# Attention with a shared key/value head and a Fourier block: probability-times-value bursts over six, five and five key chunks, with half sums kept in DRAM

## The chip, the cores and the metric

The kernel runs on one core of one Trainium2 chip. The metric is the device time of one execution in microseconds (us), lower is better. TensorE (PE) multiplies matrices, VectorE (DVE), ScalarE (ACT) and GpSimd (POOL) work on vectors, SyncE (SP) issues the DMAs. In the profile PEld stands for PE's weight loads, which overlap its matmuls, and a "q" behind an engine's name for its sequencer.

## What is computed

Two independent results stand side by side in the output. The left half is attention with 32 heads of 32 columns over 2048 positions, where all heads share one key and one value head. The right half is the real part of a two-dimensional Fourier transform, written as matrix products.

```python
# left half; x: 1 x 2048 x 1024
q = (x @ wq).reshape(B, S, H, Dh).transpose(0, 2, 1, 3)
k, v = x @ wk, x @ wv
scores = jnp.einsum("bhqd,bkd->bhqk", q, k) * (Dh ** -0.5)
p = softmax(scores, axis=-1)
o = jnp.einsum("bhqk,bkd->bhqd", p, v)
a = o.transpose(0, 2, 1, 3).reshape(B, S, H * Dh) @ wo
# right half; its own x
a_, b_ = einsum("bsd,ed->bse", x, dft_hid_re), einsum("bsd,ed->bse", x, dft_hid_im)
y = einsum("ts,bse->bte", dft_seq_re, a_) - einsum("ts,bse->bte", dft_seq_im, b_)
```

## The kernel before

**Products of three.** The projections, the Fourier stages and the output product are "groups". A group sums 8 blocks of 128 rows (stage one of the Fourier block: 4) into one PSUM bank `psb`; each block is three matmuls, since both operands are split into a high and a low part (`rh`, `rl` and `mh`, `ml`) to keep the precision. One such matmul is called a fill here. Operands come through two lines (`RL` for the right side, `ML` for the left) of four steps: load by SP (`r`, `m`), combination of two or three loaded tiles by POOL (`comb`), rounding to the high part (`hi_r`, `hi_m`) and subtraction to the low part (`lo`), on POOL after the start. Each step has a lead, counted in fills ahead of the operand's use, and `pump` issues what is due after every fill. A load can start when a buffer of the tile is free: three for the first source, two for the second; a third source had tiles of the pool `hp`.

**Stage two.** Seven products in turn (`PRODUCTS`), each of two halves of eight groups. The first half's sums are kept in eight tiles `h` of the pool `hp`; in the second half DVE adds the bank to `h`, and POOL adds `h` to the running results `y`, which are loaded from DRAM before (`load_y`, six buffers) and stored behind it.

**Attention.** It goes through 32 units, a unit being 4 heads by 512 queries, and each unit through 32 steps. A step of the main loop issues, in this order: the scores of a later unit (two matmuls `pss`, the row maxima by DVE into `nm`, and one step later their exponential sums by ACT); the exponentials of this unit (`expo`: two matmuls `pst` of 128 keys against 1024 query columns, and ACT's exponential into a tile `p`); now and then a burst; and the step's share of fills. The scores come with their row's logarithm already subtracted: query tiles `qst` have two spare rows, 96 and 97, that hold it, and the keys `kst` hold ones there. The query tile is taken from a pool of three, and POOL clears rows 96 to 127 in every unit (`open_unit`). The logarithms of a unit are made in small steps at fixed places (`LSE`): `lse_1`, `lse_1b`, `lse_2` on DVE and ACT, a transpose on PE (`lse_3`), and DMAs into the spare rows (`lse_4`, tile `mt`); in steps of the main loop these are 21, 22, 24, 26 and 28.

**Bursts.** `pv(u, k)` multiplies the tiles `p` of four chunks of 128 keys with the values, each for four heads, in four column groups of the array, and sums them in a bank; DVE adds the bank to `ov`. A burst follows every eighth step, and `level` spreads the fills over the seven steps in between, so that their sum up to a burst is as `goal` says. Nine tiles `p` are enough for this. `aside` takes a few fills more if a group is just begun or nearly done.

**Order.** Every engine runs its instructions in the order in which the program issues them; the fills between the matmuls of attention are set by `take`. SP is a queue of its own: a load that waits for a free buffer holds up all DMAs behind it. All instructions are issued through one helper, so the profile gives them all the same line, L66, and they are told apart by the names of their tiles.

Of the kernel before, what the change touches and what calls it, by code (L numbers as in the profile page):

```python
# [8 lines left out]
F32 = mybir.dt.float32  # L9
F32R = mybir.dt.float32r  # L10
# [6 lines left out]
P = 128  # L17
# [3 lines left out]
DH = 32  # L21
W = 512
NG = 8
NQ = 4
NC = 16
# [62 lines left out]
def tile_kernel(ctx: ExitStack, tc, xT, wq, wkv, wo, xbT, wT, cT, out):  # L88
# [40 lines left out]
    mp = pool(ctx, "mp", NM, side="right")  # L129
    yp = pool(ctx, "yp", NY, side="right")  # L130
    op = pool(ctx, "op", 2, side="right")
    hp = pool(ctx, "hp", 1, side="right")

    def move(q, to, of):
        q.dma_start(to.bitcast(F32), of.bitcast(F32))


    class Line:
# [6 lines left out]
        def may(self, k):  # L145
            i = self.n[k]
            if i >= len(self.items):
                return False
            if k == 0:
                return i < min(self.n[3] + self.nstage, self.n[1] + self.nstage - 1)  # L150
            if i >= self.n[k - 1]:
                return False
            if k == 2 and i >= self.nring:
                return self.items[i - self.nring].last < pos["fill"]
            return True
# [23 lines left out]
    def load_r(it):  # L179
        if it.pre or it.t:  # L180
            return
        it.t = []
        for n, (ap, _) in enumerate(it.srcs):
            if n < 2:
                it.t.append(r0p.tile([P, W], F32, name=f"r{n}", bufs=NR0 - n))
            else:
                it.t.append(spare(0, 5))
            sp.dma_start(it.t[-1], ap())

    def load_m(it):  # L190
        if it.pre:
            return
        it.t = []
        for n, (ap, _) in enumerate(it.srcs):
            a = ap()
            if n < 2:
                t = m0p.tile([P, 4, P], F32, name=f"m{n}", bufs=NM0 - n)
            else:
                t = spare(5, 3).rearrange("p (a b) -> p a b", a=4)
            it.t.append(t[:, :a.shape[1], :a.shape[2]])  # L200
            sp.dma_start(it.t[-1], a)

    turn = {0: 0, 5: 0}

    def spare(first, n):

        turn[first] += 1
        return hp.tile([P, W], F32, name=f"h{first + turn[first] % n}")

    def comb(it):  # L210
        if it.pre:
# [105 lines left out]
    def store(to, of, key=None):  # L317
        def go():
            move(sp, to, of)
            if key:  # L320
                ready.add(key)
        soon(go)
# [159 lines left out]
    hs = {}  # L482

    def have(key, ap):
        assert key in ready, key
        return ap

    def stage2():
        seen, total = {}, {}
        for _, _, outs in PRODUCTS:  # L490
            for t, e, _ in outs:
                total[t, e] = total.get((t, e), 0) + 1
        for mt, nt, outs in PRODUCTS:
            for half in range(2):
                R = [Item([(lambda s=s, k=k: have((k, s), s_d[k][s]), -1 if nt == SUB and i else 1) for i, k in enumerate(nt)])
                     for s in range(half * 8, half * 8 + 8)]
                for k in range(8):
                    left = []
                    for q in range(2):
                        s0 = half * 8 + q * 4  # L500
                        left.append(Item([(lambda a=a, k=k, s0=s0: cT[a[0], a[1] * 8 + k, :, s0:s0 + 4], a[2]) for a in mt]))
                    if half == 0:
                        def post(ps, k=k):
                            hs[k] = hp.tile([P, W], F32, name=f"h{k}")
                            dve.tensor_copy(hs[k], ps)
                        yield Group(left, R, post)
                        continue
                    ys = []
                    plan = []
                    for t, e, sg in outs:  # L510
                        n = seen.get((t, e, k), 0)
                        seen[t, e, k] = n + 1
                        it = None
                        if n:
                            it = Item([(lambda t=t, e=e, k=k: y_d[t][e][k], 1)])
                            ys.append(it)
                        r0 = (t * 8 + k) * P
                        to = out[r0:r0 + P, D + e * W:D + (e + 1) * W] if n + 1 == total[t, e] else y_d[t][e][k]
                        plan.append((sg, it, to))

                    def post(ps, k=k, plan=plan):
                        h = hs[k]
                        dve.tensor_add(h, h, ps)
                        for sg, it, to in plan:
                            if it is not None:
                                (gp.tensor_add if sg > 0 else gp.tensor_sub)(it.y, it.y, h)
                                store(to, it.y)
                            elif sg > 0:
                                store(to, h)
                            else:  # L530
# [39 lines left out]
    rest += [o_group(b, t, e, ws) for e, ws in ((1, w1), (0, w0)) for b in range(NQ - 1) for t in range(4)]  # L570
    add(start + rest)

    qsp = pool(ctx, "qsp", 3)
    pp = pool(ctx, "pp", 9)
    sm = pool(ctx, "sm", 2)
    onp = pool(ctx, "onp", 1)

# [7 lines left out]
    def open_unit(u):  # L585
        b, g = units[u]
        assert ("q", b, g) in ready
        q = qsp.tile([P, 4, W], F32R, name="qst")
        gp.memset(q[96:P].bitcast(F32), 0.0)
        for r, src in enumerate((qh_d, ql_d, qh_d)):  # L590
            move(sp, q[r * DH:(r + 1) * DH], src[b][g].rearrange("(h d) c -> d h c", d=DH))
        qst[u] = q
        nm[u] = sm.tile([P, 10, NC], F32, name="nm")
# [64 lines left out]
    def expo(n):  # L658
# [5 lines left out]
            te.matmul(ps[:, a], kst[:, c * P:(c + 1) * P], qst[u][:, 2 * hp_ + a], start=True, stop=True)  # L664
        act.activation(pt[u, c, hp_], ps, AF.Exp)

    def pv(u, k):

        aside()
        ps = bank("psb")  # L670
        for c in range(4 * k, 4 * k + 4):
            for h in range(4):
                te.matmul(ps[h * DH:(h + 1) * DH], v[:, c], pt[u, c, h // 2][:, h % 2], start=c == 4 * k, stop=c == 4 * k + 3)
        if k == 0:
            ov[u] = onp.tile([P, W], F32, name="ov")
            dve.tensor_copy(ov[u], ps)
        else:
            dve.tensor_add(ov[u], ov[u], ps)
        cur["at"] += 1
        if k == NC // 4 - 1:  # L680
            b, g = units[u]
            hi_ = onp.tile([P, W], F32R, name="oh")
            lo_ = onp.tile([P, W], F32R, name="ol")
            lse["out"] = hi_, lo_

# [29 lines left out]
    TURN = 6  # L715
    LSE = {1: (lse_1,), 2: (lse_1b,), 4: (lse_2,), 8: (lse_4,)}

    room = [(lambda t=t, k=k: t[:, k]) for t in [pp.tile([P, 2, W], F32, name="p") for _ in range(9)] for k in range(2)]
    room += [(lambda t=t: t) for t in [hp.tile([P, W], F32, name=f"h{k}") for k in range(8)]]
# [21 lines left out]
    def goal(n):  # L741
        return PRO + (FILL - PRO - LAST - MORE * (total - QUIET)) * n // total + MORE * max(n - QUIET, 0)


    def level(n):
        k, r = divmod(n, 8)
        if r == 0:
            return
        left = goal((k + 1) * 8) - pos["fill"]
        take(left - left * (7 - r) // (8 - r))  # L750

    for n in range(total):
        u, r = divmod(n, SU)
        if n == total - 12:
            w1 = wo_set(1)
            add([o_group(NQ - 1, t, e, ws) for e, ws in ((0, w0), (1, w1)) for t in range(4)])
        score_step(n + SU + LEAD)
# [12 lines left out]
    pv(len(units) - 1, 3)  # L770
    while ends:
        ends.pop(0)()
    hi7, lo7 = lse["out"]
# [64 lines left out]
```

## Time and profile before

| | before |
|---|---|
| runs, median (lowest to highest) | 2794.53 us (2789.01 to 2796.99), 3 runs |
| profiled execution | 2791.25 us |
| its span, first to last instruction | 2789.3 us |
| mean granted clock of PE | 0.998 |
| busy: PE, ACT, POOL, DVE | 99%, 78%, 59%, 58% |
| share of the DMA engines' time | 51.6% |

The span is one execution. "Busy" counts the time in which an engine has an instruction under way; PE's matmuls overlap, and PE is hardly ever idle. The largest groups of PE's instructions (mean length of one, which contains the overlap):

```profile
L66 PE MATMUL psb<-rh,mh 128*128 128x512 f32 (+1 forms) x1852 | 730.4, 394 | 9.7 <-ACT rh L66 8.3
...
L66 PE MATMUL pss<-kst,qst 128*128 128x512 f32 x2048 | 657.1, 402 | 1.3 <-ACT pss L66 1.2
L66 PE MATMUL pst<-qst,kst 128*128 128x512 f32 x2048 | 649.5, 398 | 4.4 <-DMA qst<-mt 3.6
...
L66 PE MATMUL psb<-p,v 128*32 128x512 f32 x4096 | 466.3, 596 | 0.0
```

A row reads: line, engine, operation, output tile from input tiles, shapes, number; busy us and mean ns of one; idle time of the engine just before them, and what ended it. The trace has each matmul of a burst twice, 32 for the 16 that the program issues.

### The profile page before, as it was taken

How to read it: one execution, taken by the hardware profiler on the slowest of the kernel's cores; microseconds unless marked ns; L12 is line 12 of the kernel's file. 1: busy time of each engine (PE TensorE's matmuls, PEld its weight loads, DVE VectorE, ACT ScalarE, POOL GpSimd, SP SyncE). 2: the span in 40 equal slices, each digit the busy share in tenths (PEclk: the TensorE clock that was granted, in tenths of full speed). 3: DMA queues.
4: the chain of work that ended last, by engine and by line, in shares of the span. 5: the costliest groups of instructions: out<-in, count | busy, mean ns of one | idle time of the engine just before them, and what ended most of it. 6: DMA issues, size and time to landing. Idle time of an engine off the chain costs nothing.

```text
span 2789.3 us, 40153 instructions
## 1 busy us (share of the span) xinstructions
PE 2763.8 (99%) x13904; PEld 1932.7 (69%) x13904; DVE 1624.4 (58%) x1864; ACT 2181.4 (78%) x3151; POOL 1651.0 (59%) x1622
## 2 busy tenths in 40 slices
PE   8999999999999999999999999999999999999999
PEld 5876767667666767666676767667676767676666
DVE  6766666666676665555555655555565555555411
ACT  4578888888788888888888888878888888888740
POOL 3755534665535538767686567798887885640110
PEclk9999999999999999999999999999999999999999
DMA  7544325766576554545453454555564552554455
GB/s 253 197 140 129 110 103 174 242 213 203 189 237 212 171 175 156 162 144 153 143 189 104 129 167 139 160 198 162 163 193 150 167 160 80 159 163 140 126 166 173
DMA packets 304203, 459.87 MB, mean 165 GB/s; under 512 B 32128, under 2 KB 97152, under 8 KB 304000
## 3 DMA queue, kind: packets, MB, share of 16 engines
q1 hardware_dynamic: 304000, 457.30, 51.6%
q8 instruction: 110, 1.80, 0.3%
q14 instruction: 93, 0.76, 0.1%
HBM read 351.54 MB, written 104.60 MB: 164 GB/s over the span
## 4 chain that ended last, share of the span: by engine, by line
PE 96%; DMA 1%; DVE 1%; ACT 1%; issue 0%; POOL 0%; SPq 0%; ACTq 0%; POOLq 0%; DVEq 0%
PE psb L66 61%; PE pss L66 18%; PE pst L66 17%; DMA p<-in_xT_dram 0%; DVE nm L66 0%; ACT pss L66 0%; SPq L66 0%; DVE rl L66 0%; ACT p L66 0%; DMA r<-s 0%; ACT rh L66 0%; DMA qst<-mt 0%; DMA ql<-ql 0%; DMA r<-in_xT_dram 0%; POOL ml L66 0%
## 5 line engine op out<-in xcount | busy, mean ns | idle before, releaser
L66 DVE TENSOR_REDUCE nm<-pss 128x1 f32<-128x1024 f32 x1024 | 1252.7, 1223 | 591.2 <-PE pss L66 590.3
L66 ACT ACTIVATE p<-pst 128x1024 f32<-128x1024 f32 x1024 | 1052.2, 1028 | 463.8 <-PE pst L66 461.3
L66 ACT ACTIVATE pss<-pss,nm 128x1024 f32<-128x1024 f32 x1024 | 1112.9, 1087 | 67.3 <-DVE nm L66 65.9
L66 PE MATMUL psb<-rh,mh 128*128 128x512 f32 (+1 forms) x1852 | 730.4, 394 | 9.7 <-ACT rh L66 8.3
L66 PE MATMUL psb<-rh,ml 128*128 128x512 f32 (+1 forms) x1852 | 730.1, 394 | 2.2 <-POOL ml L66 2.2
L66 PE MATMUL psb<-rl,mh 128*128 128x512 f32 (+1 forms) x1852 | 728.5, 393 | 0.3 <-DVE rl L66 0.3
L66 PE MATMUL pss<-kst,qst 128*128 128x512 f32 x2048 | 657.1, 402 | 1.3 <-ACT pss L66 1.2
L66 PE MATMUL pst<-qst,kst 128*128 128x512 f32 x2048 | 649.5, 398 | 4.4 <-DMA qst<-mt 3.6
L66 PEld LDWEIGHTS pss<-kst,qst 128*128 128x128 f32 x2048 | 372.2, 188 | 184.7 <-issue 102.3
L66 POOL TENSOR_TENSOR ml<-m,mh 128x512 fp32r<-128x512 f32 x340 | 438.8, 1291 | 48.2 <-ACT mh L66 40.4
L66 PE MATMUL psb<-p,v 128*32 128x512 f32 x4096 | 466.3, 596 | 0.0
L66 PEld LDWEIGHTS pst<-qst,kst 128*128 128x128 f32 x2048 | 377.4, 188 | 112.2 <-ACT p L66 20.8
L66 PEld LDWEIGHTS psb<-rh,mh 128*128 128x128 f32 (+1 forms) x1852 | 346.7, 187 | 95.9 <-ACT rh L66 9.0
L66 PEld LDWEIGHTS psb<-rh,ml 128*128 128x128 f32 (+1 forms) x1852 | 346.6, 187 | 86.7 <-POOL ml L66 3.5
L66 PEld LDWEIGHTS psb<-rl,mh 128*128 128x128 f32 (+1 forms) x1852 | 346.7, 187 | 84.5 <-DVE rl L66 1.4
L66 PEld LDWEIGHTS psb<-p,v 128*32 128x32 f32 x4096 | 120.0, 109 | 276.6 <-issue 265.6
L66 POOL CAST mh<-m 128x512 fp32r<-128x512 f32 x339 | 208.1, 614 | 166.0 <-PE psb L66 145.3
L66 POOL TENSOR_TENSOR r<-r,r 128x512 f32<-128x512 f32 x112 | 144.4, 1289 | 271.6 <-DMA r<-s 135.2
L66 POOL CAST rh<-r 128x512 fp32r<-128x512 f32 x214 | 131.5, 614 | 262.0 <-PE psb L66 144.9
L66 POOL TENSOR_TENSOR rl<-r,rh 128x512 fp32r<-128x512 f32 x214 | 276.2, 1291 | 3.9
L66 POOL TENSOR_TENSOR m<-m,m 128x512 f32<-128x512 f32 x192 | 247.9, 1291 | 28.7 <-DMA m<-in_xbT_dram 20.6
L66 DVE TENSOR_TENSOR ov<-ov,psb 128x512 f32<-128x512 f32 x96 | 66.0, 688 | 272.0 <-PE psb L66 272.0
(68 smaller groups left out, 929.5 us busy)
## 6 DMA issues: line engine op xcount, KB each, us to landing
m<-in_cT_dram SPq DMA_DIRECT2D x384, 256.0 KB, 3.7
r<-s SPq DMA_DIRECT2D x192, 256.0 KB, 4.3
y<-y SPq DMA_DIRECT2D x96, 256.0 KB, 4.6
r<-in_wT_dram SPq DMA_DIRECT2D x80, 256.0 KB, 3.7
m<-in_xbT_dram SPq DMA_DIRECT2D x80, 256.0 KB, 4.2
y<-u SPq DMA_DIRECT2D x80, 256.0 KB, 2.8
m<-in_wq_dram SPq DMA_DIRECT2D x64, 256.0 KB, 3.0
qst<-qh SPq DMA_DIRECT2D x64, 256.0 KB, 5.5
```

Source lines behind the costliest of these rows:

```text
L66: return lambda *a, **k: self.tc.keep_in_program_order(f(*a, **k))
```

## The change

A unit's 16 key chunks are cut at 0, 6, 11 and 16: three bursts a unit, at steps 12, 22 and 0 of the next, and `level` spreads the fills up to the next of these steps. Thirteen tiles `p` hold six chunks and one step. The room for four more tiles is that of `hp`, which goes: the half sums of stage two are copied to a tile of the output pool, stored to DRAM, and loaded in the second half as one more item of the `y` line; third sources share the second source's two buffers, and an item with three sources (or the one behind it) is loaded only after the item ahead has been combined. The three query tiles are named once; POOL clears the spare rows in the first three units alone, and later units get zeros into rows 96 and 97 by a small DMA from rows of `kst` that stay zero.

```diff
-    hp = pool(ctx, "hp", 1, side="right")
@@ class Line, may
             if k == 0:
+                if self.n[1] < i and any(len(it.srcs) > 2 for it in self.items[i - 1:i + 1] if it.srcs):
+                    return False
                 return i < min(self.n[3] + self.nstage, self.n[1] + self.nstage - 1)
@@ load_r
-            if n < 2:
-                it.t.append(r0p.tile([P, W], F32, name=f"r{n}", bufs=NR0 - n))
-            else:
-                it.t.append(spare(0, 5))
+            k = min(n, 1)
+            it.t.append(r0p.tile([P, W], F32, name=f"r{k}", bufs=NR0 - k))
             sp.dma_start(it.t[-1], ap())
@@ load_m
...
+            k = min(n, 1)
+            t = m0p.tile([P, 4, P], F32, name=f"m{k}", bufs=NM0 - k)
@@ stage2
-        for mt, nt, outs in PRODUCTS:
+        for f, (mt, nt, outs) in enumerate(PRODUCTS):
+            hs = [dram.tile([P, W], F32, name=f"hs_{f}_{k}") for k in range(8)]
...
-                        def post(ps, k=k):
-                            hs[k] = hp.tile([P, W], F32, name=f"h{k}")
-                            dve.tensor_copy(hs[k], ps)
+                        def post(ps, k=k, hs=hs, f=f):
+                            o = op.tile([P, W], F32, name="qh")
+                            dve.tensor_copy(o, ps)
+                            store(hs[k], o, ("h", f, k))
...
-                    ys = []
+                    part = Item([(lambda k=k, hs=hs, f=f: have(("h", f, k), hs[k]), 1)])
+                    ys = [part]
...
-                    def post(ps, k=k, plan=plan):
-                        h = hs[k]
+                    def post(ps, part=part, plan=plan):
+                        h = part.y
                         dve.tensor_add(h, h, ps)
@@ pools of attention
-    qsp = pool(ctx, "qsp", 3)
-    pp = pool(ctx, "pp", 9)
+    qsp = pool(ctx, "qsp", 1)
+    rows = []
+    NP = 13
+    pp = pool(ctx, "pp", NP)
@@ open_unit
-        q = qsp.tile([P, 4, W], F32R, name="qst")
-        gp.memset(q[96:P].bitcast(F32), 0.0)
+        if u < 3:
+            rows.append(qsp.tile([P, 4, W], F32R, name=f"qst{u}"))
+            gp.memset(rows[u][96:P].bitcast(F32), 0.0)
+        q = rows[u % 3]
+        if u >= 3:
+            move(sp, q[96:98].rearrange("p a b -> p (a b)"), kst[98:100])
@@ pv
+    CUT = (0, 6, 11, NC)
...
-        for c in range(4 * k, 4 * k + 4):
+        for c in range(CUT[k], CUT[k + 1]):
...
-        if k == NC // 4 - 1:
+        if k == len(CUT) - 2:
@@ level
-        k, r = divmod(n, 8)
-        if r == 0:
+        r = n % SU
+        if r in ENDS:
             return
-        left = goal((k + 1) * 8) - pos["fill"]
-        take(left - left * (7 - r) // (8 - r))
+        more = min(e for e in ENDS if e > r) - r
+        left = goal(n + more) - pos["fill"]
+        take(left - left * (more - 1) // more)
@@ main loop, with ENDS = [2 * c for c in CUT]
-        if r % 8 == 0 and n:
-            pv(*divmod(n // 8 - 1, 4))
+        if r in ENDS and n:
+            pv((n - 1) // SU, (ENDS.index(r) - 1) % (len(CUT) - 1))
```

How the instructions move is seen best in three places. The first is PE's order at the end of the sixth unit, steps 30 and 31, ahead of the burst of its last chunks; a step begins with `pss` and `pst`, and the rows of `psb` are its fills. Before:

```order
L66 MATMUL pss<-kst,qst 128x512 x2
L66 MATMUL pst<-qst,kst 128x512 x2
L66 MATMUL psb<-rh,ml 128x512
L66 MATMUL psb<-rh,mh 128x512
L66 MATMUL psb<-rl,mh 128x512
L66 MATMUL psb<-rh,ml 128x512
L66 MATMUL psb<-rh,mh 128x512
L66 MATMUL pss<-kst,qst 128x512 x2
L66 MATMUL pst<-qst,kst 128x512 x2
L66 MATMUL psb<-rl,mh 128x512
L66 MATMUL psb<-rh,ml 128x512
L66 MATMUL psb<-rh,mh 128x512
```

And now:

```order
L66 MATMUL pss<-kst,qst_1499 128x512 x2
L66 MATMUL pst<-qst_2184,kst 128x512 x2
L66 MATMUL psb<-rh,ml 128x512
L66 MATMUL psb<-rh,mh 128x512
L66 MATMUL psb<-rl,mh 128x512
L66 MATMUL psb<-rh,ml 128x512
L66 MATMUL pss<-kst,qst_1499 128x512 x2
L66 MATMUL pst<-qst_2184,kst 128x512 x2
L66 MATMUL psb<-rh,mh 128x512
L66 MATMUL psb<-rl,mh 128x512
L66 MATMUL psb<-rh,ml 128x512
L66 MATMUL psb<-rh,mh 128x512
```

Five fills a step there have become four, in five steps in a row; over the whole program, steps of four fills without a burst go from 42 to 82, those of five from 570 to 651, those of six from 266 to 170.

The second is DVE's order where `lse_2` ends (the reciprocal), in the sixth unit; `ov` is the add of a burst, `y` that of a group of stage one. Before:

```order
L66 TENSOR_REDUCE md<-nm 128x16 x2
L66 TENSOR_REDUCE nm<-nm 128x16 x2
L66 TENSOR_REDUCE l<-md 128x16
L66 RECIPROCAL nm<-l 128x16
L66 TENSOR_TENSOR y_6014<-y_6014,psb 128x512
L66 TENSOR_TENSOR ov<-ov,psb 128x512
L66 TENSOR_REDUCE nm<-pss 128x1
```

And now:

```order
L66 TENSOR_REDUCE md<-nm 128x16 x2
L66 TENSOR_REDUCE nm<-nm 128x16 x2
L66 TENSOR_REDUCE l<-md 128x16
L66 RECIPROCAL nm<-l 128x16
L66 TENSOR_TENSOR y_6028<-y_6028,psb 128x512
L66 TENSOR_REDUCE nm<-pss 128x1
```

The burst that stood between `lse_2` and the next row maxima has gone two steps ahead, to step 22. In 10 of the 32 units a group's sum stands directly behind the reciprocal now, in one of them two instructions.

The third is SP's order in the second half of stage two's fourth product, around group 4 (`s00` and `s01` are sources of `r` for the product after it; a `y_` on the left is a store of the group before). Before:

```order
L66 DMA m0_17462<-in_cT_dram 128x512
L66 DMA m1_17464<-in_cT_dram 128x512
L66 DMA y0_17487<-y_0_0_4_245 128x512
L66 DMA y0_17489<-y_0_1_4_253 128x512
L66 DMA r0_17511<-s00_5_323 128x512
L66 DMA r1_17513<-s01_5_339 128x512
L66 DMA m0_17516<-in_cT_dram 128x512
L66 DMA m1_17518<-in_cT_dram 128x512
L66 DMA y_0_0_3_244<-y0_17337 128x512
```

And now:

```order
L66 DMA m0_17519<-in_cT_dram 128x512
L66 DMA m1_17521<-in_cT_dram 128x512
L66 DMA y0_17544<-hs_3_4_407 128x512
L66 DMA y0_17546<-y_0_0_4_245 128x512
L66 DMA y0_17548<-y_0_1_4_253 128x512
L66 DMA r0_17580<-s00_5_320 128x512
L66 DMA r1_17582<-s01_5_336 128x512
L66 DMA m0_17585<-in_cT_dram 128x512
L66 DMA m1_17587<-in_cT_dram 128x512
L66 DMA y_0_0_3_244<-y0_17396 128x512
```

The load of the half sum `hs` stands ahead of the two `y` loads, and so ahead of the two loads of `r`.

More of the change, by code (lines that the diff above doesn't have):

```diff
@@ L195, in load_m @@
             a = ap()
[L196 to L199, printed above, removed]
+            k = min(n, 1)
+            t = m0p.tile([P, 4, P], F32, name=f"m{k}", bufs=NM0 - k)
             it.t.append(t[:, :a.shape[1], :a.shape[2]])
             sp.dma_start(it.t[-1], a)
[L203 to L208, printed above, removed]
     def comb(it):
@@ L480, in stage1 @@
                     yield Group(left, R[n], post, ys=ys, part=(R, 4 * n))
-    hs = {}
     def have(key, ap):
@@ L670, in pv @@
         ps = bank("psb")
-        for c in range(4 * k, 4 * k + 4):
+        for c in range(CUT[k], CUT[k + 1]):
             for h in range(4):
-                te.matmul(ps[h * DH:(h + 1) * DH], v[:, c], pt[u, c, h // 2][:, h % 2], start=c == 4 * k, stop=c == 4 * k + 3)
+                te.matmul(ps[h * DH:(h + 1) * DH], v[:, c], pt[u, c, h // 2][:, h % 2], start=c == CUT[k], stop=c == CUT[k + 1] - 1)
         if k == 0:
@@ L716, in tile_kernel @@
     LSE = {1: (lse_1,), 2: (lse_1b,), 4: (lse_2,), 8: (lse_4,)}
-    room = [(lambda t=t, k=k: t[:, k]) for t in [pp.tile([P, 2, W], F32, name="p") for _ in range(9)] for k in range(2)]
-    room += [(lambda t=t: t) for t in [hp.tile([P, W], F32, name=f"h{k}") for k in range(8)]]
+    room = [(lambda t=t, k=k: t[:, k]) for t in [pp.tile([P, 2, W], F32, name="p") for _ in range(NP)] for k in range(2)]
     for n, (it, to) in enumerate(zip(RL.items, room)):
@@ L742, in goal @@
         return PRO + (FILL - PRO - LAST - MORE * (total - QUIET)) * n // total + MORE * max(n - QUIET, 0)
+    ENDS = [2 * c for c in CUT]
     def level(n):
-        k, r = divmod(n, 8)
-        if r == 0:
+        r = n % SU
+        if r in ENDS:
             return
-        left = goal((k + 1) * 8) - pos["fill"]
-        take(left - left * (7 - r) // (8 - r))
+        more = min(e for e in ENDS if e > r) - r
+        left = goal(n + more) - pos["fill"]
+        take(left - left * (more - 1) // more)
     for n in range(total):
@@ L769, in tile_kernel @@
     take(last[0].at - pos["fill"] - 12)
-    pv(len(units) - 1, 3)
+    pv(len(units) - 1, len(CUT) - 2)
     while ends:
```

## The prediction

> **What bounds the kernel now.** On the page I read the chain of work that ended last first, as shares of the span by engine.
>
> ```profile
> PE 96%; DMA 1%; DVE 1%; ACT 1%; issue 0%; POOL 0%; SPq 0%; ACTq 0%; POOLq 0%; DVEq 0%
> ```
>
> PE (TensorE) carries 96% of the chain that ended last: a term counts if it changes PE's work or makes PE wait. The next view is the timeline of PE over one step and one burst (start, length, instruction; matmuls overlap, so starts are compared, not lengths).
>
> ```profile
> 1201.67 0.40 PE L66 MATMUL psb<-rh,mh 128*128 128x512 f32 x1
> ...
> 1202.37 0.63 PE L66 MATMUL pst<-qst,kst 128*128 128x512 f32 x2
> ...
> 1203.76 0.39 PE L66 MATMUL psb<-rh,ml 128*128 128x512 f32 x1
> 1204.08 3.64 PE L66 MATMUL psb<-p,v 128*32 128x512 f32 x32
> ...
> 1208.22 0.63 PE L66 MATMUL pst<-qst,kst 128*128 128x512 f32 x2
> ```
>
> A step's last fill (a product from the groups) is followed by the next pst 0.70 us later (1201.67 to 1202.37); with a burst in between it is 4.46 us (1203.76 to 1208.22). A burst costs 3.76 us. Its inside is seen on the weight loads:
>
> ```profile
> 1204.53 0.13 PEld L66 LDWEIGHTS psb<-p,v 128*32 128x32 f32 x4 [0.30 <-issue]
> ...
> 1206.68 0.13 PEld L66 LDWEIGHTS psb<-p,v 128*32 128x32 f32 x4 [0.30 <-issue]
> ```
>
> Five intervals take 2.15 us, so a set of four concurrent matmuls takes 0.43 us; the trace has 32 matmuls, eight sets, 3.44 us. The other **0.32 us is paid once per burst**, on entering and leaving it.
>
> **The change, part by part.**
>
> *Bursts (PE).* The sets stay the same, 32 per unit, now as 12, 10 and 10 where it was four times 8. One entry and exit less per unit: 32 x 0.32 = **-10.2 us**. That longer bursts pay the same 0.32 isn't shown before; nothing in the rows grows with the number of sets except the sets. The 32 adds on ov that go with them lie beside PE's work and count nothing.
>
> *Fills per step (ACT).* A unit keeps its 153 or 154 fills, but they spread over 29 steps without a burst where it was 28, so more steps have only four. A step with four asks ACT for the same two exponentials in less time. Of PE's timeline the rows of pst alone: a burst step that nothing had delayed, and the last steps ahead of a burst and that burst's own:
>
> ```profile
> 1061.24 0.62 PE L66 MATMUL pst<-qst,kst 128*128 128x512 f32 x2
> 1065.94 0.63 PE L66 MATMUL pst<-qst,kst 128*128 128x512 f32 x2
> ...
> 1113.88 0.63 PE L66 MATMUL pst<-qst,kst 128*128 128x512 f32 x2
> 1115.97 0.63 PE L66 MATMUL pst<-qst,kst 128*128 128x512 f32 x2
> 1117.83 0.63 PE L66 MATMUL pst<-qst,kst 128*128 128x512 f32 x2
> 1119.73 0.73 PE L66 MATMUL pst<-qst,kst 128*128 128x512 f32 x2
> 1121.74 0.73 PE L66 MATMUL pst<-qst,kst 128*128 128x512 f32 x2
> 1126.54 0.63 PE L66 MATMUL pst<-qst,kst 128*128 128x512 f32 x2
> ```
>
> A step of five fills takes 2.09 us (from 1113.88). The three of four fills behind it take 1.86, 1.90 and 2.01 us, and the burst step that follows 4.80 where the undisturbed one takes 4.70: the first is free, the second loses 0.04, each further one 0.15, the burst 0.10. So a run of one costs nothing, of two 0.14, of three 0.29, of four 0.44, of five 0.59. Counted in the order of PE's instructions, the kernel before has 42 such steps (13 runs of one, 10 of two, 3 of three: 2.3 us), the changed one 82 (9, 11, 8, 3 of four, 3 of five: 7.0 us). Difference **+4.7 us**. Runs of four and five don't occur before; the bound below is that they cost no more than three (+3), above that each such step loses all of 2.09 - 1.86 (+7). I take the straight continuation, since 2.01 us is already ACT's own pace.
>
> *The log-sum (DVE).* lse_2 ran under a burst (step 24); the burst now stands at step 22.
>
> ```profile
> 1202.57 1.22 DVE L66 TENSOR_REDUCE nm<-pss 128x1 f32<-128x1024 f32 x1 [0.86 <-PE pss L66]
> 1022.51 0.27 DVE L66 TENSOR_REDUCE md<-nm 128x16 f32<-128x32 f32 x2
> ...
> 1023.40 0.63 DVE L66 TENSOR_TENSOR y<-y,psb 128x512 f32<-128x512 f32 x1
> ```
>
> DVE idles 0.86 us per step; lse_2 takes 0.89 (1022.51 to 1023.40), so alone it just fits. With a group's sum behind it, 0.63 more, the next row maxima start 0.66 us late, of which ACT and PE together absorb some 0.3 (what the first two steps of four fills showed). By DVE's order this meets 10 units; in 8 of them step 24 has six fills, 0.23 us longer, which absorbs the rest. Two units at 0.4 and one with two instructions behind it at 0.6: **+1.4 us** (0 to 4).
>
> *Half sums through DRAM.* 56 stores and 56 loads more on SP's queue, 256 KB each. What can suffer is what stands behind them, so I looked for the stretch in which PE isn't covered. Two windows, one half product each in stage two (columns: length, then busy us and count for PE, PEld, DVE, ACT, POOL; granted clock, DMA share, GB/s), and two rows of the waits inside the long one:
>
> ```profile
> 1760.00:1869.00 109.00, 103.22 (x515) 70.80 (x514) 59.11 (x64) 84.61 (x122) 94.23 (x89) 0.98 0.61 196
> 1869.00:1970.00 101.00, 101.00 (x516) 70.55 (x515) 58.77 (x65) 84.34 (x123) 86.21 (x84) 1.00 0.50 159
> POOL r L66 <- DMA r<-s: 14.6, 6, 3.8
> PE pst L66 <- DMA qst<-mt: 3.6, 1, 3.6
> ```
>
> The second half of the fourth product takes 8 us more than the half product behind it, with POOL at its busiest. The chain of waits there runs around a loop:
>
> ```profile
> 1834.64 0.43 SPq L66
> 1835.12 5.30 DMA r<-s
> 1840.56 0.14 POOL r L66
> ```
>
> POOL's subtraction (ml) frees a buffer, SP may then issue m, y and r loads in a row, r lands, POOL adds it and comes to the next ml. The change puts the half sum's load ahead of each pair of r loads in all eight groups. Its price lies between SP's issue, 0.47 us (1834.64 to 1835.12), and what 256 KB need at the fullest rate of the trace, 0.88 us (294 GB/s in the window 1848.50 quoted below); I take 0.63, between them. POOL waited for r six times: 6 x 0.63 = **+3.8 us**. Bounds: -2, if POOL's lag shrinks instead, and +9, if all eight pay both.
>
> DVE then needs that load for its add on h. Group 4 of this half:
>
> ```profile
> 1820.32 0.90 SPq L66 DMA_DIRECT2D y<-y  x2
> 1823.95 0.69 DVE L66 TENSOR_TENSOR h<-h,psb 128x512 f32<-128x512 f32 x1
> y<-y SPq DMA_DIRECT2D x96, 256.0 KB, 4.6
> ```
>
> The half sum takes the place of the first y load: issued at 1820.32, landed 4.6 us later (the page's median) at 1824.9, 1.0 us after DVE could have added. The row maxima, ACT and PE stand behind this. With the 0.63 of the loop it is about **+1.5 us** for this group (0 to 4, with its neighbour). In half zero the sum is copied to a tile of two buffers and stored; the same buffer is wanted two groups, some 48 fills or eight steps, later, and a transfer of this size lands in 4.6 us: nothing.
>
> *Rows cleared once (POOL).* 29 clears go, 29 small DMAs come, ahead of each unit's query loads.
>
> ```profile
> 1808.94 1.80 POOL L66 MEMSET qst<- 32x2048 f32 x1
> 1814.54 1.29 POOL L66 TENSOR_TENSOR r<-r,r 128x512 f32<-128x512 f32 x1 [3.80 <-DMA r<-s]
> ```
>
> In the only stretch where POOL is short, the clear is followed by 3.80 us of waiting for r: its 1.80 us are covered by that wait, so **0** (-1.8 at best). In the window behind it POOL is busy 86 of 101 us and no wait of PE rests on it.
>
> *Sum:* -10.2 + 4.7 + 1.4 + 3.8 + 1.5 = **+1.2 us** on the profiled execution's 2791.25: 2792.5. That execution lies 3.3 us under the median of the runs, 2794.53; I add half of it: **2794 us**.
>
> **A rule on the clock.** In the long window PE waits 3.6 us at a unit's start, for the DMA of mt:
>
> ```profile
> 1848.50:1852.00 3.50, 0.30 (x2) 0.00 (x0) 1.22 (x1) 0.84 (x2) 3.50 (x4) 1.00 0.88 294
> 1852.00:1855.50 3.50, 3.10 (x9) 1.69 (x13) 0.59 (x1) 1.88 (x2) 1.85 (x3) 0.52 0.65 210
> ```
>
> Right behind it the granted clock is 0.52 for 3.5 us, about 1.7 us lost. The Trainium skill (TensorE: Matmul & The Clock Gate, Part 1) says that PE falls to half its clock after an idle window of some 3.4 us and comes back after a busy window of the same length; the trace agrees, with one such event. By that rule a somewhat shorter wait there would save the 1.7 us as well, and every further wait of that length costs them again.
>
> **Rivals.**
>
> *Faster: the loop in the fourth product loosens.* Longer bursts give POOL pauses of 5.5 us to catch up, and the clears are gone; if r then lands in time, the 8 us go: -10.2 + 4.7 - 8 = -13.5, **2779 us** with the half of 3.3. For it: the loop misses by little (109 against 101). Against: the pauses per unit are the same in sum, and the clear was covered.
>
> *Slower: the half sum's load holds DVE.* Place: DVE's add on h in second halves. A group of 24 fills takes four steps of six, 4 x (2.09 + 0.23) = 9.3 us, at the least; so it decides from the point where SP lags by 9.3 - 4.6 = 4.7 us, and in group 4 above it lagged by 1.0 more. If 16 groups of the POOL-heavy products each wait 1.0 us, the case's own lateness, that is +16 in place of +1.5, **2810 us**. A further unit start that waits 3.6 us and loses 1.7 to the clock would add 5.3. Against: before, only that stretch shows PE waiting.
>
> *The saving isn't per burst.* If the 0.32 us grow with the number of sets, nothing is saved: +11.4, **2804 us**. Against: the two ends are seen as ends.
>
> **How the numbers follow.** Forecast 0.62, loosened loop 0.18, held DVE 0.16, no saving 0.04. 0.3% of 2794.53 is 8.4 us, about what a measurement of this kernel can tell from no change: faster is below 2786.1, slower above 2802.9. The first rival is faster (0.18), the last two slower (0.20), the rest the same (0.62). The lower bounds of the terms sum to about -9 (2784), the upper to +14 (2807); the range of 2784 to 2806 holds these and leaves out the far part of both rivals.
>
> **What would show it.** 96 bursts at 3.76 us for eight sets, 4.6 for ten and 5.5 for twelve; runs of four and five steps with four fills at 2.01 us each; the fourth product's second half above 109 us; DVE waiting on a load from the half sums, there only. I am wrong if that window comes out near 101 us, or if DVE's wait for half sums adds up to over 10 us in stage two, or if the fixed part of a burst differs.

## The result and the profile after

| | before | after |
|---|---|---|
| runs beside each other, median (lowest to highest) | 2792.85 us (2789.01 to 2796.99), 4 runs | 2807.07 us (2805.45 to 2811.13), 4 runs |
| ratio, 95% interval | | 1.0054 (1.0042 to 1.0067) |
| span of the profiled execution | 2789.3 us | 2809.3 us |
| mean granted clock of PE | 0.998 | 0.996 |

The changed kernel is 14 us (0.5%) longer. Its profiled execution took 2811.13 us, the longest of its four, so what is read from that trace can be some 4 us more than the median. The chain of work that ended last, by engine, says where to look: PE's share of it was 96%, and what came in is transfers, POOL and SP's queue.

```profile
PE 89%; DMA 5%; POOL 2%; issue 2%; SPq 1%; ACT 1%; DVE 1%; POOLq 0%; ACTq 0%; DVEq 0%
```

Next the waits of the whole span (columns: what waited, what released it, us in all, number of waits, the longest), those rows that answer to the rows of before, and two new ones.

```profile
POOL r L66 <- DMA r<-s: 172.1, 59, 12.6
PE pst L66 <- DMA qst<-mt: 11.2, 5, 4.4
PE psb L66 <- POOL ml L66: 6.4, 4, 2.3
PE psb L66 <- POOL mh L66: 3.5, 2, 1.9
DVE y L66 <- DMA y<-hs: 0.8, 2, 0.5
```

Before, the first row read 135.2 us in 56 waits. DVE waits for half sums 0.8 us in all: the load that was to hold DVE comes in time. PE itself waits little, 21 us in these rows, against 5.8 before. Now the windows, one product of stage two each (length, then busy us and count for PE, PEld, DVE, ACT, POOL; granted clock, DMA share, GB/s). Four of before, the second to the fifth product:

```profile
1257.00:1458.00 201.00, 201.00 (x1027) 140.28 (x1026) 118.03 (x137) 167.93 (x244) 154.23 (x151) 1.00 0.50 159
1458.00:1659.00 201.00, 201.00 (x1028) 140.53 (x1027) 117.09 (x127) 168.35 (x243) 124.07 (x125) 1.00 0.43 132
1659.00:1869.00 210.00, 204.22 (x1031) 141.56 (x1030) 119.39 (x137) 169.02 (x246) 164.66 (x159) 0.99 0.52 164
1869.00:2070.00 201.00, 201.00 (x1027) 140.44 (x1026) 117.18 (x127) 167.70 (x243) 171.79 (x165) 1.00 0.56 175
```

And of after, the second to the sixth:

```profile
1253.00:1463.00 210.00, 205.38 (x1046) 141.57 (x1045) 117.70 (x135) 168.74 (x246) 150.20 (x148) 0.99 0.55 172
1463.00:1662.00 199.00, 199.00 (x1013) 140.66 (x1012) 115.23 (x124) 167.72 (x243) 117.52 (x122) 1.00 0.50 154
1662.00:1879.00 217.00, 208.42 (x1045) 142.80 (x1044) 117.43 (x135) 168.17 (x244) 164.60 (x160) 0.98 0.58 184
1879.00:2078.00 199.00, 198.23 (x1010) 140.22 (x1009) 114.66 (x123) 167.11 (x243) 161.42 (x156) 1.00 0.59 188
2078.00:2293.00 215.00, 206.80 (x1046) 142.20 (x1045) 117.79 (x135) 168.19 (x245) 167.38 (x164) 0.98 0.56 175
```

Before, one product is long. After, three are, the second, fourth and sixth, and in each of them PE has gaps of 5 to 9 us and a lower clock, while POOL is no busier. To see which half, and how near the others come, take from the trace the start of every 192nd fill (the length of a half product) and, for each tile `ml`, the time from the end of POOL's subtraction to the first fill that uses it: POOL's lead over PE, of which the smallest in a half counts.

| half product | length before | after | smallest lead before | after |
|---|---|---|---|---|
| 2nd, second half | 100.5 us | 108.4 us | 4.3 us | 0.1 us |
| 4th, second half | 108.8 | 115.4 | 0.1 | 0.1 |
| 5th, second half | 100.5 | 96.5 | 3.8 | 2.3 |
| 6th, first half | 100.8 | 104.0 | 5.0 | 1.7 |
| 6th, second half | 100.8 | 110.7 | 3.3 | 0.1 |
| all 14 | 1417.1 | 1443.9 | | |

The other halves add up to the same within 4 us; what lies behind stage two, to PE's last matmul, came out 5.2 us shorter (312.6 to 307.4), stage one 4.1 shorter, and what lies ahead of stage one 2.7 longer (340.3 to 343.0). Most of these three is only where the borders fall among the bursts: by the end of stage two the changed kernel has done six sets of a burst and two steps' scores and exponentials more than the kernel before, an estimated 4.4 us of PE's work (0.43 us a set, 0.93 a step), and by the start of stage one four sets and one step more, some 2.6 us. Single halves shift in the same way. So the measure for the table is a run in which nothing is lost: with r loaded earlier (below), the same five halves of the changed kernel take 101.1, 101.1, 95.5, 102.3 and 101.3 us. Against this it loses 7.3, 14.3, 1.0, 1.7 and 9.4.

How the lead is lost is seen in the second half of the second product. SP's queue (start, us it took, the DMA) and POOL at the same time:

```profile
1396.04 0.81 SPq L66 DMA_DIRECT2D m<-in_cT_dram  x2
1396.89 0.43 SPq L66 DMA_DIRECT2D y<-hs  x1
1397.37 0.43 SPq L66 DMA_DIRECT2D y<-y  x1
1397.90 0.63 SPq L66 DMA_DIRECT2D qst<-kst  x1
1398.57 0.39 SPq L66 DMA_DIRECT2D qst<-qh  x1
1399.00 0.44 SPq L66 DMA_DIRECT2D qst<-ql  x1
1399.49 0.43 SPq L66 DMA_DIRECT2D qst<-qh  x1
1399.96 2.44 SPq L66 DMA_DIRECT2D r<-s  x2
```

```profile
1400.28 1.29 POOL L66 TENSOR_TENSOR ml<-m,mh 128x512 fp32r<-128x512 f32 x1
1409.32 1.29 POOL L66 TENSOR_TENSOR r<-r,r 128x512 f32<-128x512 f32 x1 [7.75 <-DMA r<-s]
```

The chain of waits in the same stretch, and how long such a load took before (the page's list of DMA issues; the last column is the median from issue to landing, us):

```profile
1396.42 5.63 DMA m<-in_cT_dram
...
1402.06 7.13 DMA r<-s
```

```profile
r<-s SPq DMA_DIRECT2D x192, 256.0 KB, 4.3
```

A subtraction frees a buffer, SP issues all that had piled up behind it, the half sum ahead of the r loads, and the second r load, last in the row, lands 7.13 us after its issue, where 4.3 was the median before. Its issue is late too: by the chain it comes at 1402.06, when the second of the m loads, issued at 1396.42, has landed. POOL stands still for 7.75 us, more than the 4.3 us by which it led PE at the least before. In the run below in which the half sums' loads bring two rows only, the same row of DMAs ends with that r issued 4.6 us after the first m load, where it is 6.0 here, and POOL stands still for 5.23 us.

Where PE then waits, the clock follows. A unit start in the fourth product, two windows:

```profile
1855.00:1859.00 4.00, 0.45 (x2) 0.01 (x1) 1.23 (x1) 0.98 (x2) 3.83 (x4) 1.00 0.89 308
1859.00:1863.00 4.00, 3.15 (x9) 1.69 (x13) 0.59 (x1) 1.92 (x3) 2.22 (x3) 0.54 0.85 255
```

PE's wait for `mt` here is 4.4 us; `mt` is queued on SP behind the same loads (DVE had it ready at 1842.56, SP issued it at 1854.46, behind an m load that had waited for a buffer, the half sum and two `y`). There are four stretches at half clock in stage two, 20.5 us in all, where before it was one of 3.4: 3.4 us in the second half of the second product, 3.4 and 6.8 in that of the fourth, 6.8 in that of the sixth. If PE loses half of such a stretch at the most, that is up to 10.2 us of the changed kernel's time, and 1.7 of the one before.

### The profile page after: what moved, and what is told of

Same layout as the page of the kernel before. It is cut to its first block, busy times and chain, and to the rows that moved or that the text cites. A ratio compares the mean times of both kernels' runs of the same rounds, so it can differ in the third digit from the quotient of the medians.

```text
span 2809.3 us, 40359 instructions
## 1 busy us (share of the span) xinstructions
PE 2767.0 (98%) x13904; PEld 1936.5 (69%) x13904; DVE 1601.6 (57%) x1832; ACT 2176.8 (77%) x3151; POOL 1598.2 (57%) x1593
## 4 chain that ended last, share of the span: by engine, by line
PE 89%; DMA 5%; POOL 2%; issue 2%; SPq 1%; ACT 1%; DVE 1%; POOLq 0%; ACTq 0%; DVEq 0%
PE psb L66 56%; PE pss L66 17%; PE pst L66 16%; DMA r<-s 2%; SPq L66 1%; POOL ml L66 1%; DMA qst<-mt 1%; POOL mh L66 0%; DMA p<-in_xT_dram 0%; ACT pss L66 0%; DMA m<-in_cT_dram 0%; POOL rh L66 0%; DMA r<-in_xT_dram 0%; ACT p L66 0%; DMA ql<-ql 0%
## 5 line engine op out<-in xcount | busy, mean ns | idle before, releaser
L66 POOL TENSOR_TENSOR r<-r,r 128x512 f32<-128x512 f32 x120 | 154.7, 1290 | 315.3 <-DMA r<-s 172.1
L66 POOL TENSOR_TENSOR m<-m,m 128x512 f32<-128x512 f32 x200 | 258.5, 1293 | 31.7 <-DMA m<-in_xbT_dram 19.6
L66 ACT ACTIVATION_READ_ACCUMULATOR pss<-pss,nm 128x1 f32 x1024 | 210.5, 206 | 0.0
```

The lines of the kernel that those rows point to most:

```text
L66: return lambda *a, **k: self.tc.keep_in_program_order(f(*a, **k))
```

## The experiments

Each comparison is a ratio to the kernel before, run on the same chip, with its 95% interval; the medians of before in the three sets of runs were 2792.05 to 2792.56 us. "Half 4b" is the second half of the fourth product, and so on.

### The trip alone, and the rest alone

The changed kernel with the old bursts:

```diff
-    NP = 13
+    NP = 9
...
-    CUT = (0, 6, 11, NC)
+    CUT = (0, 4, 8, 12, NC)
```

> The change with bursts of four chunks and nine tiles p again; the half sums' trip through DRAM and the rows cleared once stay. Theory A (the trip alone makes the loop of POOL, SP and the r loads too slow): the saving of the bursts and their price at ACT go (+10.2 - 4.7), the losses in stage two stay, some 2810 us, with the second, fourth and sixth products still 8 to 13 us longer than the others. Theory B (the long bursts make the demand for operands uneven, and only with them the loop falls behind): the losses go, 2793 to 2797 us, with the fourth product alone long, as before.

Measured: 2813.16 us, 1.0083 (1.0068 to 1.0098). Half 4b takes 114.8 us, 5b 106.9, 6b 105.8, the others 100.6 as before. The losses don't need long bursts; these only shift where POOL runs out of lead (2b and 6b with them, 5b and 6b without). The total is not a clean price: with fewer tiles `p` and no `h`, only 18 of 26 first operands were loaded ahead, and the first 144 fills took 49.8 us where it was 43.1 (10.2 us of them at half clock, where it was 3.4).

The changed kernel without the trip; the half sum is not stored and not loaded, and DVE copies the bank where it added:

```diff
-                            store(hs[k], o, ("h", f, k))
...
-                    part = Item([(lambda k=k, hs=hs, f=f: have(("h", f, k), hs[k]), 1)])
+                    part = Item(None)
...
-                        dve.tensor_add(h, h, ps)
+                        dve.tensor_copy(h, ps)
```

> The change without the 56 stores and 56 loads of half sums: the second half's sum is copied where it was added, so the right half of the output lacks the first halves; all else stays. Theory A: stage two loses what it loses to the trip, so some 25 us less than the change, 2780 to 2786 us. Theory B: the transfers have little share, 2800 to 2807 us. If both are needed, it comes out between, with the fourth product still long at 209 us or more.

Measured: 2788.26 us, 0.9990 (0.9981 to 0.9999). The trip costs 2807.07 - 2788.26 = 18.8 us. Half 2b is 101.1 and 6b 102.5; 4b stays long at 111.1. POOL's smallest lead is 1.5 us in 2b and 0.5 in 6b even so: the rest of the change has used up some 3 us of it, and the trip takes what is left. The long bursts are the likely cause (with bursts of four and the trip, above, 2b keeps 2.3 us), but the half sums also hold a buffer of the `y` line here and the rows are cleared by DMA, and no run takes the bursts alone away.

### Stores, transfer, or place in the queue

Only the load left out, the store kept (the rest as above):

> The change with the half sums' 56 stores kept and their 56 loads left out; the second half copies its sum where it was added, so the right half of the output lacks the first halves. Theory A1 (the load in front of r, in the second halves, costs): 2788 to 2791 us, as without the trip. Theory A2 (the transfers as such, stores too, take time from other DMAs): about half of the 19 us comes back, 2796 to 2800 us.

Measured: 2787.82 us, 0.9982 (0.9972 to 0.9991). The 56 stores cost nothing; the 56 loads cost all.

The load kept in its place, but for two of the 128 rows:

```diff
-        sp.dma_start(it.y, it.srcs[0][0]())
+        n = 2 if it.small else P
+        sp.dma_start(it.y[0:n], it.srcs[0][0]()[0:n])
...
+                    part.small = True
...
-                        dve.tensor_add(h, h, ps)
+                        dve.tensor_copy(h, ps)
```

> The changed kernel, but the load of a half sum brings two of its 128 rows (4 KB for 256 KB) and DVE copies the bank where it added; SP's queue has every instruction in the same place. The loads cost 19 us in all. Theory A (the transfer's time on the DMA engines, in which the r loads behind it run later, is the price): 2788, as with the loads left out; POOL's wait for r in all near 150 us. Theory B (the place in SP's queue is the price: one more issue of 0.47 us, and one more wait for a free buffer ahead of r): 2805 to 2808, wait for r near 172. Both in part: in between.

Measured: 2787.22 us, 0.9981 (0.9972 to 0.9990). SP issues the same DMAs in the same order, and the loss is gone: half 2b 101.1, 4b 108.5, 6b 102.1. Its waits show it too, beside the 172.1 above:

```profile
POOL r L66 <- DMA r<-s: 132.7, 54, 12.4
```

So what costs is the 256 KB under way ahead of r, and not the instruction's place and time on SP; where that traffic makes SP wait too, as for the second r load above, the wait comes of the bytes. That DVE copies in these three runs where it added takes away only its wait for half sums, 0.8 us in all.

### Taking the link away

r loaded 56 fills ahead instead of 40, in the changed kernel:

```diff
-    RL = Line(NR0, NR, (40, 40, 14, 8), load_r, comb, hi_r, lo)
+    RL = Line(NR0, NR, (56, 40, 14, 8), load_r, comb, hi_r, lo)
```

> The change with the r loads issued 16 fills earlier (lead 56 where POOL's combination keeps 40), so that POOL doesn't come to the r add before the load has landed. If POOL's wait for r is the link of the loop that fails, its 172 us shrink to under 60 and the losses of stage two go: 2778 to 2788 us. If SP's lag behind POOL's m buffers is the link, r is as late as before and the time stays at 2803 to 2807 us.

Measured: 2781.13 us, 0.9961 (0.9947 to 0.9976). POOL's wait for r and the windows of the fourth and the sixth product in this run:

```profile
POOL r L66 <- DMA r<-s: 27.6, 7, 11.2
```

```profile
1649.00:1852.00 203.00, 203.00 (x1045) 141.55 (x1044) 117.62 (x135) 168.15 (x246) 164.85 (x160) 1.00 0.62 193
...
2050.00:2253.00 203.00, 203.00 (x1043) 140.28 (x1042) 116.97 (x135) 167.74 (x245) 163.27 (x158) 1.00 0.60 186
```

217 and 215 us have become 203, PE is never idle there, the clock is 1.00, and more is moved per second, not less. All of stage two takes 1410.2 us, and POOL's smallest lead is 4.0 us or more but for 3.1 in half 5a. The trip is still there in full. So the link that failed is r's arrival, and no other loss is left in stage two that these rows show.

The same edit in the kernel before:

> The kernel before with the same earlier r loads. If POOL's wait for r is the link, the fourth product's 8 us go: 2782 to 2787 us. If not, 2791 to 2795 us.

Measured: 2784.33 us, 0.9973 (0.9963 to 0.9982). Half 4b falls from 108.8 to 100.5 us. With r early in both, the change is worth 2781.13 - 2784.33 = -3.2 us (no run of the one, 2777.2 to 2781.5, reaches those of the other, 2782.9 to 2785.4).

And with r early, bursts of four in the changed kernel (CUT and NP as above):

> The change with r loads 16 fills earlier, and bursts of four chunks again. Without losses in stage two, this against the same with 6, 5, 5 (2781.1 us) is what the bursts bring: by my terms 10.2 - 4.7 - 1.4 = 4.1 us, so 2785 us; 2791 if the 0.32 us per burst is the whole of it. Against the kernel before with r early (2784.3) it is what the trip and the rows cost when r isn't in the loop: 0 by the theory, so 2784 to 2786 us.

Measured: 2792.42 us, 0.9999 (0.9990 to 1.0009). Stage two is as short as in the kernel before with r early (1409.0 us both), so the trip and the rows cost nothing once r comes early. The total is 7 us over the expectation; 6 of them lie in the first 144 fills again (48.7 us against 42.3, with 10.2 us at half clock against 3.4).

### The half sum behind r

The load of the half sum 14 fills ahead of its group instead of 24, behind the group's r and m loads (`ahead` is the lead of an item of the `y` line, 24 for all others):

```diff
...
+                    part.ahead = 14
-                    ys = [part]
+                    ys = []
...
+                    ys.append(part)
```

> The change with the half sum's load moved 10 fills back in SP's order, behind the pair of r loads and the m loads; the same transfers, the same lengths. Theory A1 (what counts is that r stands behind it): most of the 19 us come back, 2788 to 2794 us, unless DVE has to wait for the half sum (then up to 2800, with rows of DVE waiting for that load). Theory A2 (the transfers as such): 2803 to 2808 us.

Measured: 2810.64 us, 1.0066 (1.0051 to 1.0081), no gain. POOL's lead comes back (3.5 us or more in halves 2b, 4b and 6b; its wait for r falls to 141.9), but a new row stands among the waits:

```profile
DVE y L66 <- DMA y<-hs: 41.0, 16, 5.5
```

The longest of them, on DVE's timeline, where idle time and its end stand in brackets:

```profile
1875.47 1.22 DVE L66 TENSOR_REDUCE nm<-pss 128x1 f32<-128x1024 f32 x1 [0.85 <-PE pss L66]
1882.21 0.69 DVE L66 TENSOR_TENSOR y<-y,psb 128x512 f32<-128x512 f32 x1 [5.52 <-DMA y<-hs]
1882.81 2.35 DVE L66 TENSOR_REDUCE nm<-pss 128x1 f32<-128x1024 f32 x2
```

```profile
1877.15 4.88 DMA y<-hs
...
1882.89 1.15 DVE nm L66
...
1884.12 1.21 ACT pss L66 x2
1885.38 1.22 PE pss L66 x2
```

DVE waits for the half sum with the row maxima queued behind its add; the chain then runs through ACT into PE, and half 5a takes 109.6 us, where it is 102.9 with r early. This is the held DVE of the prediction, made by moving the load later. Behind r the load is too late, ahead of r at 40 fills it makes r too late; of what was tried, only more lead for r helps both. The run doesn't show what the order alone is worth, since the two losses overlap.

### The terms that the loss had covered

r early, and the clear of the spare rows back in every unit:

```diff
-    qsp = pool(ctx, "qsp", 1)
+    qsp = pool(ctx, "qsp", 3)
...
-        if u < 3:
-            rows.append(qsp.tile([P, 4, W], F32R, name=f"qst{u}"))
-            gp.memset(rows[u][96:P].bitcast(F32), 0.0)
-        q = rows[u % 3]
-        if u >= 3:
-            move(sp, q[96:98].rearrange("p a b -> p (a b)"), kst[98:100])
+        q = qsp.tile([P, 4, W], F32R, name="qst")
+        gp.memset(q[96:P].bitcast(F32), 0.0)
```

> The changed kernel with r loaded at 56 fills and, in addition, the clear of the query tile's spare rows back in every unit (29 x 1.80 us more on POOL, 29 small DMAs less). Theory (the clear lies in POOL's slack): 2781, within 2 us of the run without it, no half product of stage two above 104. Rival (POOL has no slack in the products with three sources; about a dozen unit starts lie there): 12 x 1.8 = 22 us at most, 2790 to 2803, with the second halves of the second, fourth and sixth product above 104 again.

Measured: 2780.70 us, 0.9959 (0.9947 to 0.9972): 0.4 us from the run without it.

The same clear in the changed kernel as it is, r at 40 fills:

> The changed kernel (r at 40 fills) with the clear of the spare rows back in every unit. Theory (the prediction's: the clear is covered by POOL's wait for r): 2807, within 3 us. Rival (in the three halves in which the loop through POOL, SP and r sets the pace each clear costs its 1.8 us: 4 or 5 unit starts, two of them hit PE): 2811 to 2816.

Measured: 2809.29 us, 1.0065 (1.0052 to 1.0078): 2.2 us over 2807.07, with the two intervals overlapping, and in the profiled executions stage two is 2.3 us shorter. No price can be seen either way, down to the 2 or 3 us that these runs can tell.

Steps of four fills made to stand apart, in the changed kernel with r early (`take(left - left * (more - 1) // more)` rounds up, so that the fours gather ahead of a burst; here it rounds to the nearest number, which leaves 72 such steps of the 82, in 56 runs of one, 2 of two and 3 of four):

```diff
-        take(left - left * (more - 1) // more)
+        take((2 * left + more) // (2 * more))
```

> The change with r loads 16 fills earlier, and the fills of a window rounded to the nearest number instead of up, so that steps of four fills stand singly among those of five: in PE's order 56 runs of one, 2 of two, 3 of four, where there were 9, 11, 8, 3 and 3 of five. If a single step of four is free, as the steps of the kernel before say, this takes 7.0 - 1.6 = 5.4 us off: 2775 to 2777 us. If each step of four costs the same wherever it stands, nothing: 2780 to 2782 us.

Measured: 2776.65 us, 0.9946 (0.9930 to 0.9963), 4.5 us less than with r early alone. This is the shortest of all the kernels here, below both that the study began with.

Both edits in the kernel before:

> The kernel before with r loaded at 56 fills and the fills spread by rounding to the nearest number, so that its 42 steps of four fills all stand alone (13 runs of one, 10 of two, 3 of three before). If the loss in runs of four-fill steps is as the prediction priced it: 2784.3 - 2.3 = 2782. If it is nothing at such short runs: 2784. Against the changed kernel with both edits (2776.7) it should then be 5 to 8 us longer, which is what long bursts are worth once r comes in time.

Measured: 2781.96 us, 0.9964 (0.9950 to 0.9978), 2.4 us less than with r early alone. Long bursts with everything that comes with them are then worth 2776.65 - 2781.96 = -5.3 us; the two were run in different sets, and again no run of the one reaches the other's (2775.7 to 2779.3, 2780.3 to 2783.2).

## Why the prediction was wrong

**Size and place were missed in one part of the sum.** The forecast was no change, 2794 us; the time came out at 2807, 1 us above the range. The two terms of the half sums' trip, +3.8 and +1.5, should have been 18.8, more than the +9 and +4 of their upper bounds. None of the three signs named for being wrong came: the window did not come out near 101 us, DVE's wait for half sums stayed under 10, and the fixed part of a burst did not change. All three looked at places that the prediction had already priced.

**The step that failed** is the one that begins "What can suffer is what stands behind them, so I looked for the stretch in which PE isn't covered". It took the halves in which PE did not wait before as free of charge, and priced the load in one half only, 4b. But eight groups at the 0.63 us of the prediction are 5.0 us, and POOL's lead in the trace of before was 4.3 us in 2b, 3.8 in 5b and 3.3 in 6b. With 4b these are the second halves in which both m and the r of the next product are sums of two loads (`PRODUCTS`). The prediction's own price was above the lead in three more halves; the lead was in the trace and was not read. Two of the three ran out, 2b and 6b; with bursts of four it was 5b and 6b. So the comparison names the places at risk, but not which of them fall.

The runs give 2b and 6b 7.3 and 8.2 us, after against the kernel without the trip. That is more than 5.0 less the lead, for two reasons: the rest of the change had left only 1.5 and 0.5 us of lead, and in both halves PE's waits brought the half clock, for 3.4 and 6.8 us. With half of these taken off, an estimate for a load is (7.3 - 1.7 + 1.5) / 8 = 0.9 us in 2b and (8.2 - 3.4 + 0.5) / 8 = 0.7 in 6b, where the prediction took 0.63 between bounds of 0.47 and 0.88.

In 4b, where the price was set, it can't be told closely. Half 4b takes 115.4 us, and 111.1, 108.5 and 106.9 in the three runs without the transfer, which follow the half clock in them, 6.8, 3.4 and 0 us. So the price is 4.3 to 8.5 us with the clock in it, and an estimated 2.6 to 3.5 without, where 5.3 was predicted. The clock had no term in the sum, though the prediction names its 1.7 us for an event.

**What the price is made of** was half right. It was set between SP's issue and the transfer's time. With two rows instead of 128 the issue stays and the loss goes: it is the bytes.

**The held DVE** was mis-sized: the term of +1.5 was 0.8 us of waiting in all. The rival built on it came near the time, 2810, by luck (its own sum gives 2809) and by the wrong mechanism: in the changed kernel the loads come in time, and only in the run with the load behind r does DVE wait (16 times, 41.0 us).

**Bursts** were right. Two of them on PE's timeline, ten sets (40 records) and twelve (48), between a last fill and the next pst:

```profile
1200.94 0.39 PE L66 MATMUL psb<-rh,ml 128*128 128x512 f32 x1
1201.26 4.50 PE L66 MATMUL psb<-p,v 128*32 128x512 f32 x40
...
1206.26 0.63 PE L66 MATMUL pst<-qst,kst 128*128 128x512 f32 x2
...
1229.53 0.40 PE L66 MATMUL psb<-rh,ml 128*128 128x512 f32 x1
1229.86 5.36 PE L66 MATMUL psb<-p,v 128*32 128x512 f32 x48
...
1235.72 0.63 PE L66 MATMUL pst<-qst,kst 128*128 128x512 f32 x2
```

5.32 and 6.19 us, less the 0.70 of a step without a burst, are 4.62 and 5.49: ten and twelve times 0.43, and 0.32 or 0.33 once. The rival without a saving falls.

**Steps of four fills** were right. A run of five, and the start of the step behind it, by the rows of pst:

```profile
464.78 0.63 PE L66 MATMUL pst<-qst,kst 128*128 128x512 f32 x2
466.64 0.63 PE L66 MATMUL pst<-qst,kst 128*128 128x512 f32 x2
468.54 0.74 PE L66 MATMUL pst<-qst,kst 128*128 128x512 f32 x2
470.55 0.74 PE L66 MATMUL pst<-qst,kst 128*128 128x512 f32 x2
472.56 0.73 PE L66 MATMUL pst<-qst,kst 128*128 128x512 f32 x2
474.57 0.73 PE L66 MATMUL pst<-qst,kst 128*128 128x512 f32 x2
```

1.86, 1.90 and then 2.01 us three times, as continued from runs of three. Spreading the fours should have brought back 5.4 us in the changed kernel and 2.3 in the one before, and brought 4.5 and 2.4.

**The sum of bursts, fours and log-sum** was -10.2 + 4.7 + 1.4 = -4.1; with r early in both kernels it is -3.2. That they agree so well is in part luck: in these two profiled executions what lies ahead of stage one is 5.7 us longer in the changed kernel, of which the border explains some 2.6, and for the rest the sum has no term and no run shows the cause. The log-sum's 1.4 was not measured by itself. **Rows cleared once** was put at 0, and two runs show no price.

**The loosened loop** didn't come: in the three runs with long bursts and without the transfer half 4b takes 106.9 to 111.1 us (108.8 before), and without the trip the lead in 2b and 6b shrinks. Whether long bursts alone use it up, and why, wasn't tried by itself.

**The rule on the clock** said that a somewhat shorter wait would save the 1.7 us. In the changed kernel it doesn't: a wait of 2.0 us was followed by the half clock as well (shown in the last section).

## What to carry to other kernels

A wait of 0 on the bound engine says nothing of how near the next stage is to being late. Before a load is added to a queue, measure in every stretch how far the producer is ahead of the engine that sets the end, and set the load's whole price in that stretch (number of loads times transfer time) against it: here eight times 0.63 to 0.88 us, 5 to 7 us, against 4.3, 3.8 and 3.3. A lead below the price is a warning; two of these three ran out. When a loop does run late, an earlier issue of the operand that lands last (r, 16 fills more lead) was worth 26 us in the changed kernel and 8 in the one before, for one number in the code; moving the added load back instead handed the wait to another engine.

## What was not expected of the hardware

The place in SP's queue was free, the bytes were not: the same 56 DMAs with 4 KB instead of 256 KB cost 20 us less (2787.2 against 2807.1). And a wait shorter than the 3.6 us of before can bring the half clock. Around a unit start in the second product PE waited 2.0 us for `mt`, was busy 1.99 of 4 us, and ran at 0.57 in the next window:

```profile
1442.00:1446.00 4.00, 1.99 (x10) 1.33 (x9) 2.27 (x2) 2.12 (x3) 3.58 (x3) 1.00 0.76 258
1446.00:1450.00 4.00, 4.00 (x19) 1.13 (x23) 0.69 (x1) 2.12 (x3) 2.82 (x3) 0.57 0.66 221
```

The traces suggest what counts. Every stretch at half clock in stage two lasts 3.4 or 6.8 us, one or two windows of 3.4. In the window ahead of each, PE was busy for 0.02 of it before, and for 0.41, 0.21, 0.00 and 0.45 after; no other window at full clock in stage two of these two traces, all with 0.55 or more, was followed by one. So here it was the busy share of a window, and not the length of a single wait, that went with the half clock.
